# Score products of a sliding-window attention cut from 64x64 to 64x32 tiles of the TensorE array

## The chip, the cores and the metric

The kernel runs on one core of one Trainium2 chip. The metric is the device time of one execution in microseconds (us); lower is better. Times are medians over several runs, and profile pages and traces are of one profiled execution.

Five engines work side by side, each through its own list of instructions: PE (TensorE, matmuls; its weight loads are listed as PEld), DVE (VectorE), ACT (ScalarE), POOL (GpSimd) and SP, which here issues most DMAs. They wait for each other through semaphores. Matmul results go to PSUM, from where DVE and ACT read them.

## The reference

Two independent parts fill the two halves of the output's columns.

- **A, attention.** `x` is 2048x576. `qkv = x @ wqkv`, 32 heads of 18 features. Scores `q·k * 18**-0.5` are kept where `0 <= query - key < 256`; softmax over the keys, product with `v`, heads concatenated, `@ wo`.
- **B, a long convolution.** A filter of 2048 taps for each of 576 channels is computed from 128 complex exponentials, and `u` is convolved with it by Fourier transforms of length 4096; `u * Dskip` is added.

```python
scores = jnp.einsum("bhqd,bhkd->bhqk", q, k) * (Dh ** -0.5)
mask = (idx[:, None] - idx[None, :] >= 0) & (idx[:, None] - idx[None, :] < W)   # W = 256
p = _softmax(jnp.where(mask[None, None], scores, -1e9), axis=-1)
o = jnp.einsum("bhqk,bhkd->bhqd", p, v)
```

## The kernel before

The program has no loops at run time: Python writes every instruction out. Work is split into streams (generators), and the strings of `PLAN` give by hand the order in which the streams take their steps; each engine meets its instructions in that order. There are four stretches: `front` and `tables` (about 0 to 400 us: projections of q, k, v; the tables of the convolution filter), then `first` and `rest` (attention, the convolution's transforms, and the product with `wo`).

Attention is cut into 16 sets `i`: four chunks `c` of 512 queries by four groups `o` of eight heads. For a set, `Q` (128 x 4 x 512), `K` (128 x 4 x 768; 256 keys of the chunk before, and 512 of its own) and `V` are loaded. Heads sit at partitions 0 to 63 and 64 to 127 (index `r`), four to each (indices `b`, `pp`). q and k are kept as a high and a low float16 part, so that a head has 54 rows (and a 55th for its maximum).

Three streams use them:

- `smax` (letter `s` of the plan, method `smax1`): for every block of 64 queries (`qb`) and every `pp`, one **slot** of PSUM (`ring`, three buffers of 128 x 2 x 512) gets the scores of four heads: queries on PSUM's partitions, their keys along the free axis, 320 of them (64 queries and the 256 keys before), fewer at the start of the sequence. Four matmuls (L832) with `Q` as the weights, then four more (L840, or L843 at the start of the sequence) that add -3e38 through an identity `idb` where a key may not be seen. DVE then takes the maximum of each row (L866). After 16 slots the 128 x 32 maxima are transposed (L848) and written by DMA into the 55th row of `Q`.
- `scores` (`a`, method `score1`): the same scores turned round, keys on the partitions and queries along the free axis, 55 rows, so that the maximum is subtracted by the product itself. A slot holds one to three key blocks (table `TB`), four matmuls each (L917, `K` as the weights), masks (L926), and ACT's exponential (L932), which leaves `P` in SBUF.
- `pv` (`v`): the product of `V` and `P`, float32, on tiles of 64 rows by 32 columns (L952), into `po`.

The slice `z = 64 * (r ^ b)` puts the four matmuls of a group on four different quarters (64x64) of PE's array. The convolution's steps, which the plan sets between these, are L671 (64 rows by 32 columns), L704 (32 by 64) and L765 (128 by 64). A group of matmuls here is a set of them on different tiles of the array, issued one behind the other.

```python
for b in range(2):
    for r in range(2):
        z = 64 * (r ^ b)
        rr = slice(64 * r, 64 * r + 54)
        nc.tensor.matmul(ps[z:z + 64, b, :n], d["Q"][rr, 2 * b + pp, 64 * qb:64 * qb + 64],
                         d["K"][rr, 2 * b + pp, k0:k1], start=True, stop=False, skip_group_check=True)
```

Of the kernel before, what the change touches and what calls it, by code (L numbers as in the profile page):

```python
# [42 lines left out]
def constants():  # L43
    c = {}
    tau = 2 * np.pi
    l1, l2, f1, f2 = np.arange(64), np.arange(32), np.arange(64), np.arange(32)
    ph = -tau * np.outer(l1, f1 + 0.25) / 64
    m = np.stack([np.cos(ph), np.sin(ph)], 2).reshape(64, 128)
    wu = np.concatenate([m, m])
    wk = np.tile(m.reshape(32, 2, 128), (4, 1, 1))  # L50
    w2 = np.zeros((2, 2, 32, 8, 2, 2, 64))
    i1 = np.zeros((4, 32, 8, 2, 2, 64))
    for f in range(64):
        t, s, b = f // 8, f // 4 % 2, f % 4
        ph = -tau * np.outer(l2, f + 0.25 + 64 * f2) / 2048
        co, si = np.cos(ph), np.sin(ph)
        q, r = b // 2, b % 2
        w2[r, 0, :, t, s, q] = np.concatenate([co, si], 1)
        w2[r, 1, :, t, s, q] = np.concatenate([-si, co], 1)
        i1[b ^ s, :, t, s, 0] = np.concatenate([co.T, -si.T], 1)  # L60
        i1[b ^ s, :, t, s, 1] = np.concatenate([si.T, co.T], 1)
    ph = tau * np.outer(f1 + 0.25, l1) / 64
    i2 = np.stack([np.cos(ph), -np.sin(ph)], 1) / 2048
    i2 = i2[[f ^ (f // 4 % 2) for f in range(64)]].reshape(128, 64)
    mult = {"c_cm": np.arange(64), "c_ct": np.arange(32) + 0.5, "c_ca": np.r_[64 * np.arange(8), 512 * np.arange(4)],
            "c_cp": np.r_[np.zeros(8), np.full(4, 31.5)]}
    for nm, v in mult.items():
        t = np.zeros((3, GC, GC, len(v)))
        for g in range(GC):
            t[:, g, g] = v  # L70
        c[nm] = t.reshape(96, GC, len(v))
    big = -3e38
    p, x = np.arange(64)[:, None], np.arange(64)[None]
    sm = np.concatenate([np.where(x <= p, big, 0), np.where(x > p, big, 0)], 1)
    far, near, no = np.where(x >= p, big, 0), np.where(p > x, big, 0), np.zeros((64, 64))
    tm = np.concatenate([far, near, near, far, far, no], 1)
    c["c_sm"], c["c_tm"] = np.concatenate([sm, sm]), np.concatenate([tm, tm])
    c["c_if"] = np.eye(128)
    c["c_id"] = np.concatenate([np.eye(64), np.eye(64)])
    c["c_wu"], c["c_wk"], c["c_w2"], c["c_i1"], c["c_i2"] = wu, wk, w2.reshape(128, 8, 256), i1.reshape(128, 8, 256), i2  # L80
    half = ("c_sm", "c_tm", "c_id", *mult)
    return {k: np.ascontiguousarray(v.astype(ml_dtypes.bfloat16 if k in half else np.float32)) for k, v in c.items()}
# [48 lines left out]
class Kernel:  # L131
# [667 lines left out]
    def load(self, i):  # L799
# [7 lines left out]
        t0 = 0 if c else 4  # L807
        nc.sync.dma_start(d["V"][:, t0 * 76:912], self.vd[o, :, :, 8 * c - 4 + t0:8 * c + 8].rearrange("r k t e -> (r k) (t e)"))

    def smax(self):  # L810
        for i in range(16):
            yield from self.smax1(i)

    def smax1(self, i):
        nc, (c, o), d = self.nc, divmod(i, 4), self.sets[i % 3]
        yield "PE", (d["K"],), lambda: self.loaded > i
        m = self.p["m"].tile([128, 32], F32, name="m")
        mv = m.rearrange("p (b s) -> p b s", b=2)
        for qb in range(8):
            k0 = max(64 * qb, 256 if c == 0 else 0)  # L820
            k1 = 64 * qb + 320
            n = k1 - k0
            full = n == 320
            for pp in range(2):
                if qb or pp:
                    yield "PE", (d["K"],), "ring"
                ps = self.slot()
                for b in range(2):
                    for r in range(2):
                        z = 64 * (r ^ b)  # L830
                        rr = slice(64 * r, 64 * r + 54)
                        nc.tensor.matmul(ps[z:z + 64, b, :n], d["Q"][rr, 2 * b + pp, 64 * qb:64 * qb + 64],  # L832
                                         d["K"][rr, 2 * b + pp, k0:k1], start=True, stop=False, skip_group_check=True)
                for b in range(2):
                    for r in range(2):
                        z = 64 * (r ^ b)
                        rr = slice(64 * r, 64 * r + 64)
                        if full:
                            out = ps[z:z + 64, b, :320].rearrange("p (t x) -> p t x", x=64)[:, 0:5:4]
                            nc.tensor.matmul(out, self.idb[rr], self.sm[rr], start=False, stop=True,  # L840
                                             skip_group_check=True)
                        else:
                            nc.tensor.matmul(ps[z:z + 64, b, n - 64:n], self.idb[rr], self.sm[rr, 64:],  # L843
                                             start=False, stop=True, skip_group_check=True)
                self.post("2", (ps,), lambda out=mv[:, :, 8 * pp + qb], x=ps[:, :, :n]: self.red(out, x))
        yield "PE", (m,), "ring", lambda: self.n["max"] >= 16 * i + 16
        mt = self.slot()
        nc.tensor.transpose(mt[:32, 0, :128], m, self.idf)  # L848

        def go():  # L850
            m16 = self.p["m"].tile([32, 128], F16, name="m16")
            nc.vector.tensor_scalar(m16, mt[:32, 0, :128], 2.0 ** -15, None, op0=OP.mult)
            q = d["Q"].rearrange("(h r) p n -> h r (p n)", h=2)[:, 54]

            def store():
                for b in range(2):
                    src = m16[16 * b:16 * b + 16].rearrange("s (h x) -> h s x", h=2)
                    for r in range(2):
                        nc.sync.dma_start(q[r:r + 1, 1024 * b:1024 * b + 1024].rearrange("o (s x) -> o s x", x=64),
                                          src[r ^ b])  # L860
                self.maxed = i + 1
            self.post("4", (m16,), store)
        self.post("6", (mt,), go)
# [42 lines left out]
    def score1(self, bl, d, pp, Ps):  # L906
        nc = self.nc
        ps = self.slot()
        lo = min(x[1] for x in bl)
        hi = max(x[1] + x[3] for x in bl)  # L910
        for k, (rel, off, q0, w) in enumerate(bl):
            for b in range(2):
                for r in range(2):
                    z = 64 * (r ^ b)
                    rr = slice(64 * r, 64 * r + 55)
                    kc = 64 * (rel + 4)
                    nc.tensor.matmul(ps[z:z + 64, b, off:off + w], d["K"][rr, 2 * b + pp, kc:kc + 64],  # L917
                                     d["Q"][rr, 2 * b + pp, q0:q0 + w], start=(k == 0), stop=False,
                                     skip_group_check=True)
        for blk, kinds in self.masks(bl):  # L920
            w = 64 * len(kinds)
            for b in range(2):
                for r in range(2):
                    z = 64 * (r ^ b)
                    rr = slice(64 * r, 64 * r + 64)
                    nc.tensor.matmul(ps[z:z + 64, b, 64 * blk:64 * blk + w], self.idb[rr],  # L926
                                     self.tm[rr, self.MO[kinds]:self.MO[kinds] + w], start=False, stop=True,
                                     skip_group_check=True)

        def go():  # L930
            P = self.p["P"].tile([128, 2, 512], F32, name="P")
            nc.scalar.activation(P[:, :, lo:hi], ps[:, :, lo:hi], AF.Exp, scale=self.esc)  # L932
            Ps.append(P)
        self.post("1", (ps,), go)
# [253 lines left out]
```

## Time and profile before

| | |
|---|---|
| median of 3 runs | 882.83 us (879.99 to 886.74) |
| profiled execution | span of 879.6 us; the runs lie 0.4 to 7.1 us above it, the median 3.2 |
| PE busy | 722.6 us (82%), 14234 matmuls and as many weight loads |
| DVE busy | 600.4 us (68%) |
| ACT busy | 522.5 us (59%) |
| POOL busy | 378.4 us (43%) |
| bytes moved by DMA | 150.79 MB, 171 GB/s over the span |

A profile page lists busy times of each engine and the groups of instructions behind them; the trace can be asked for the rows of a stretch of time, in which an idle time ahead of an instruction stands in brackets with what ended it. "issue" there means that the profile shows nothing that the engine waited for. A matmul's end is modelled, so that busy times of PE hold the way through the array as well; starts are what can be compared.

### The profile page before, as it was taken

How to read it: one execution, taken by the hardware profiler on the slowest of the kernel's cores; microseconds unless marked ns; L12 is line 12 of the kernel's file. 1: busy time of each engine (PE TensorE's matmuls, PEld its weight loads, DVE VectorE, ACT ScalarE, POOL GpSimd, SP SyncE). 2: the span in 40 equal slices, each digit the busy share in tenths (PEclk: the TensorE clock that was granted, in tenths of full speed). 3: DMA queues.
4: the chain of work that ended last, by engine and by line, in shares of the span. 5: the costliest groups of instructions: out<-in, count | busy, mean ns of one | idle time of the engine just before them, and what ended most of it. 6: DMA issues, size and time to landing. Idle time of an engine off the chain costs nothing.

```text
span 879.6 us, 32028 instructions
## 1 busy us (share of the span) xinstructions
PE 722.6 (82%) x14234; PEld 439.6 (50%) x14234; DVE 600.4 (68%) x797; ACT 522.5 (59%) x685; POOL 378.4 (43%) x296
## 2 busy tenths in 40 slices
PE   4565957998889789887888897778888998999986
PEld 2321523456446545465555454445555555567655
DVE  6866887887987787768767787376776778861010
ACT  3247675678777857671465565545666676676431
POOL 2266867766687655665015132032133042332020
PEclk9885969999999999995899989889999999899998
DMA  9795261557247745468559568627557684855844
GB/s 313 263 231 129 66 155 37 138 104 180 55 110 196 152 116 159 101 158 238 149 180 286 183 202 248 180 78 241 169 153 212 200 245 121 257 159 171 239 144 140
DMA packets 210763, 150.79 MB, mean 171 GB/s; under 512 B 102538, under 2 KB 191242, under 8 KB 210368
## 3 DMA queue, kind: packets, MB, share of 16 engines
q1 hardware_dynamic: 208608, 144.74, 58.2%
q0 software_dynamic: 2016, 3.99, 1.5%
q8 instruction: 112, 1.84, 0.9%
q14 instruction: 27, 0.22, 0.1%
HBM read 83.44 MB, written 65.11 MB: 169 GB/s over the span
## 4 chain that ended last, share of the span: by engine, by line
PE 49%; DVE 16%; ACT 13%; issue 11%; DMA 5%; POOL 3%; SPq 3%; ACTq 0%; DVEq 0%; POOLq 0%
PE pp L174 10%; PE po L952 7%; PE ring L174 6%; ACT P L932 5%; PE ring L917 4%; PE ring L704 4%; DVE m L866 4%; PE ring L832 3%; PE ring L671 3%; PE ring L571 2%; PE ring L449 2%; PE ring L461 2%; PE ring L765 2%; PE ring L926 1%; DVE m L548 1%
## 5 line engine op out<-in xcount | busy, mean ns | idle before, releaser
L866 DVE TENSOR_REDUCE m<-ring 128x2 f32<-128x640 f32 (+4 forms) x256 | 187.4, 779 | 59.1 <-PE ring L840 55.4
L932 ACT ACTIVATE P<-ring,esc 128x1024 f32<-128x1024 f32 (+2 forms) x160 | 166.8, 1060 | 99.2 <-PE ring L926 91.1
L542 POOL TENSOR_TENSOR m<-A,tr 128x1024 f32<-128x1024 f32 x72 | 144.0, 2019 | 78.0 <-DVE m L548 66.9
L952 PE MATMUL po<-P,V 64*32 64x320 f32 (+4 forms) x2816 | 103.4, 368 | 3.3 <-issue 3.3
L832 PE MATMUL ring<-K,Q 54*64 54x320 f16 (+4 forms) x1024 | 83.3, 327 | 23.3 <-DMA K<-kz 7.1
L986 POOL TENSOR_TENSOR osb<-osb,T 128x1024 f32<-128x1024 f32 x16 | 37.8, 2364 | 99.9 <-DVE T L981 72.4
L692 POOL TENSOR_TENSOR Y<-t,t 128x384 f32<-128x384 f32 x24 | 24.0, 1001 | 131.4 <-DVE t L687 125.4
L832 PEld LDWEIGHTS <-Q 54*64 54x64 f16 x1024 | 43.4, 111 | 69.5 <-issue 61.3
L917 PE MATMUL ring<-Q,K 55*64 55x320 f16 (+4 forms) x1408 | 68.2, 273 | 12.0 <-ACT P L932 3.2
L994 POOL TENSOR_TENSOR oh<-osb,oh 128x1024 f16<-128x1024 f32 x16 | 34.2, 2135 | 72.4 <-ACT oh L990 72.4
L174 PE MATMUL pp<-xh,wh 128*128 128x512 f16 x180 | 48.3, 400 | 18.7 <-ACT vst L361 9.4
L174 PEld LDWEIGHTS <-wh 128*128 128x128 f16 x324 | 31.8, 102 | 57.1 <-issue 18.1
L840 PE MATMUL ring<-sm,idb 64*64 64x128 bf16 x896 | 56.7, 231 | 1.3 <-issue 1.2
L548 DVE TENSOR_TENSOR m<-m,m 128x1024 f32<-128x1024 f32 x36 | 53.4, 1482 | 4.8 <-POOL m L542 4.7
L571 PE MATMUL ring<-Q,m 128*32 128x64 f32 x2304 | 42.6, 231 | 16.1 <-DVE m L548 13.4
L917 PEld LDWEIGHTS <-K 55*64 55x64 f16 x1408 | 33.8, 111 | 41.1 <-issue 32.9
L952 PEld LDWEIGHTS po<-P,V 64*32 64x32 f32 x2816 | 38.7, 108 | 30.7 <-issue 21.3
L571 PEld LDWEIGHTS ring<-Q,m 128*32 128x32 f32 x2304 | 36.9, 117 | 29.6 <-issue 11.9
L174 PE MATMUL pp<-xh,wl 128*128 128x512 f16 x180 | 49.7, 411 | 0.0
L977 DVE STREAM_TRANSPOSE T<-osb 128x1024 f32<-128x1024 f32 x16 | 19.8, 1235 | 42.3 <-ACT osb L962 42.2
L926 PE MATMUL ring<-tm,idb 64*64 64x128 bf16 (+1 forms) x1152 | 45.0, 215 | 3.7 <-issue 3.7
L523 POOL TENSOR_TENSOR tr<-tr,mab 128x768 f32<-128x768 f32 x18 | 33.6, 1868 | 31.1 <-ACT tr L518 31.0
(162 smaller groups left out, 1568.2 us busy)
## 6 DMA issues: line engine op xcount, KB each, us to landing
gx<-ust SPq DMA_DIRECT2D x16, 576.0 KB
gk<-kst SPq DMA_DIRECT2D x18, 512.0 KB
tx<-gx SPq DMA_DIRECT2D x24, 384.0 KB
tk<-gk SPq DMA_DIRECT2D x24, 384.0 KB
h<-ho SPq DMA_DIRECT2D x48, 192.0 KB
hp<-h SPq DMA_DIRECT2D x12, 768.0 KB
Q<-qz SPq DMA_DIRECT2D x16, 512.0 KB
K<-kz SPq DMA_DIRECT2D x16, 512.0 KB
```

What stands on the lines that cost most here:

```text
L174: self.nc.tensor.matmul(ps, u, v, start=(i == 0), stop=(i == len(ops) - 1))
L542: tt(m[part], A[:, ch, a0:a0 + 8].unsqueeze(3).to_broadcast(sh), tr[:, ch, part, 0:8].unsqueeze(2).to_broadcast(sh), op=OP.mult)
L548: self.nc.vector.tensor_tensor(m[0], m[0], m[1], op=OP.add)
L571: nc.tensor.matmul(kp[32 * st:32 * st + 32, j, :], m[:, ch, 32 * term:32 * term + 32], Q[:, ch, term, :], start=(term == 0), stop=(term == ...
L832: nc.tensor.matmul(ps[z:z + 64, b, :n], d["Q"][rr, 2 * b + pp, 64 * qb:64 * qb + 64], d["K"][rr, 2 * b + pp, k0:k1], start=True, stop=Fals ...
L840: nc.tensor.matmul(out, self.idb[rr], self.sm[rr], start=False, stop=True, skip_group_check=True)
L866: self.nc.vector.tensor_reduce(out, x, axis=AX.X, op=OP.max)
L917: nc.tensor.matmul(ps[z:z + 64, b, off:off + w], d["K"][rr, 2 * b + pp, kc:kc + 64], d["Q"][rr, 2 * b + pp, q0:q0 + w], start=(k == 0), st ...
L926: nc.tensor.matmul(ps[z:z + 64, b, 64 * blk:64 * blk + w], self.idb[rr], self.tm[rr, self.MO[kinds]:self.MO[kinds] + w], start=False, stop ...
L932: nc.scalar.activation(P[:, :, lo:hi], ps[:, :, lo:hi], AF.Exp, scale=self.esc)
L952: nc.tensor.matmul(po[32 * p:32 * p + 32, z, q0:q0 + w], V[64 * z:64 * z + 64, kb * 76 + 19 * p:kb * 76 + 19 * p + 32], P[p % 2][64 * z:64 ...
L986: nc.gpsimd.tensor_tensor(osb, osb, rb, op=OP.mult)
```

## The change

The four matmuls of a group become eight: each 64-wide block of weights is cut into two of 32 (index `h`), so that a group covers eight tiles of 64 rows by 32 columns, the shape that the products with `V` have. The order in a group is given by `TILES`.

- `smax1`: each half of a query block takes its own 288 keys (32 queries and the 256 before) instead of the 320 of the whole block. The mask matmuls write 2 x 32 columns of each half instead of 2 x 64. DVE's maximum runs over 288 columns. At the start of the sequence (`full` false) the keys stay as they were.
- `score1`: each key block of 64 becomes two of 32 for the same queries; the masks' weights are 32 columns of `idb`, their columns as before.
- `constants`: the table `c_sm` of the masks gets the two 32-wide parts ahead of its old second half.

The plan, the slots, the loads, and the orders of DVE, ACT, POOL and SP stay as they were.

```diff
-    sm = np.concatenate([np.where(x <= p, big, 0), np.where(x > p, big, 0)], 1)
+    y = x[:, :32]
+    sm = np.concatenate([np.where(y <= p % 32, big, 0), np.where(y > p % 32, big, 0), np.where(x > p, big, 0)], 1)
...
+    TILES = [(b, r, h) for b in range(2) for h in range(2) for r in range(2)]
...
-                for b in range(2):
-                    for r in range(2):
-                        z = 64 * (r ^ b)
-                        rr = slice(64 * r, 64 * r + 54)
-                        nc.tensor.matmul(ps[z:z + 64, b, :n], d["Q"][rr, 2 * b + pp, 64 * qb:64 * qb + 64],
-                                         d["K"][rr, 2 * b + pp, k0:k1], start=True, stop=False, skip_group_check=True)
...
+                for b, r, h in self.TILES:
+                    z, rr, q0 = 64 * (r ^ b) + 32 * h, slice(64 * r, 64 * r + 54), 64 * qb + 32 * h
+                    k0 = q0 if full else 256
+                    nc.tensor.matmul(ps[z:z + 32, b, :n], d["Q"][rr, 2 * b + pp, q0:q0 + 32],
+                                     d["K"][rr, 2 * b + pp, k0:k0 + n], start=True, stop=False, skip_group_check=True)
+                for b, r, h in self.TILES:
+                    z, rr, hh = 64 * (r ^ b) + 32 * h, slice(64 * r, 64 * r + 64), slice(32 * h, 32 * h + 32)
+                    if full:
+                        out, mk = ps[z:z + 32, b, :288].rearrange("p (t x) -> p t x", x=32)[:, 0:9:8], self.sm[rr, :64]
+                    else:
+                        out, mk = ps[z:z + 32, b, n - 64:n], self.sm[rr, 64:]
+                    nc.tensor.matmul(out, self.idb[rr, hh], mk, start=False, stop=True, skip_group_check=True)
...
-                    nc.tensor.matmul(ps[z:z + 64, b, off:off + w], d["K"][rr, 2 * b + pp, kc:kc + 64],
-                                     d["Q"][rr, 2 * b + pp, q0:q0 + w], start=(k == 0), stop=False,
-                                     skip_group_check=True)
+            for b, r, h in self.TILES:
+                z, rr, kc = 64 * (r ^ b) + 32 * h, slice(64 * r, 64 * r + 55), 64 * (rel + 4) + 32 * h
+                nc.tensor.matmul(ps[z:z + 32, b, off:off + w], d["K"][rr, 2 * b + pp, kc:kc + 32],
+                                 d["Q"][rr, 2 * b + pp, q0:q0 + w], start=(k == 0), stop=False, skip_group_check=True)
```

PE's list shows it at the end of two slots of `smax` that stand between two steps of `pv` (`po` is what `pv` writes, `sm` the mask's table; the sizes are partitions by columns of the result). Before:

```order
L840 MATMUL ring<-sm,idb 64x2x64
L840 LDWEIGHTS idb
L840 MATMUL ring<-sm,idb 64x2x64
L952 MATMUL po<-P,V_4393 32x192 x8
L832 LDWEIGHTS Q_4387
L832 MATMUL ring<-K_4388,Q_4387 64x320
```

After the change, at the same place (the line numbers of `pv` move from L952 to L942):

```order
L840 MATMUL ring<-sm,idb 32x2x32
L840 LDWEIGHTS idb
L840 MATMUL ring<-sm,idb 32x2x32
L942 MATMUL po<-P,V_4393 32x192 x8
L832 LDWEIGHTS Q_4387
L832 MATMUL ring<-K_4388,Q_4387 32x288
```

Between the `pv` step shown and the one ahead of it stood 32 rows of `smax`; now there are 64. Results of 64 partitions beside those of 32 stood there before; now all have 32. In PE's whole list there were 226 places where a score matmul of 64 columns stood next to one of `pv` or L671 with 32.

At a slot of `scores` in the same stretch, from the block of 64 columns to that of 320, before:

```order
L917 MATMUL ring<-Q_4395,K_4396 64x64
L917 LDWEIGHTS K_4396
L917 MATMUL ring<-Q_4395,K_4396 64x64
L917 LDWEIGHTS K_4396
L917 MATMUL ring<-Q_4395,K_4396 64x320
```

and after (`score1` moves from L917 to L910):

```order
L910 MATMUL ring<-Q_4395,K_4396 32x64
L910 LDWEIGHTS K_4396
L910 MATMUL ring<-Q_4395,K_4396 32x64
L910 LDWEIGHTS K_4396
L910 MATMUL ring<-Q_4395,K_4396 32x320
```

The widths stay, and each stands eight times instead of four. Over the program the score and mask matmuls go from 4608 to 9216, each with its weight load: 9216 more instructions on PE.

More of the change, by code (lines that the diff above doesn't have):

```diff
@@ L819, in smax1 @@
         for qb in range(8):
[L820 to L823, printed above, removed]
+            full = c > 0 or qb >= 4
+            n = 288 if full else 64 * qb + 64
             for pp in range(2):
@@ L827, in smax1 @@
                 ps = self.slot()
-                for b in range(2):
-                    for r in range(2):
-                        z = 64 * (r ^ b)
-                        rr = slice(64 * r, 64 * r + 54)
-                        nc.tensor.matmul(ps[z:z + 64, b, :n], d["Q"][rr, 2 * b + pp, 64 * qb:64 * qb + 64],
-                                         d["K"][rr, 2 * b + pp, k0:k1], start=True, stop=False, skip_group_check=True)
[L834 to L840, printed above, removed]
-                                             skip_group_check=True)
-                        else:
-                            nc.tensor.matmul(ps[z:z + 64, b, n - 64:n], self.idb[rr], self.sm[rr, 64:],
-                                             start=False, stop=True, skip_group_check=True)
+                for b, r, h in self.TILES:
[10 more added lines that the diff above has]
+                    nc.tensor.matmul(out, self.idb[rr, hh], mk, start=False, stop=True, skip_group_check=True)
                 self.post("2", (ps,), lambda out=mv[:, :, 8 * pp + qb], x=ps[:, :, :n]: self.red(out, x))
@@ L911, in score1 @@
         for k, (rel, off, q0, w) in enumerate(bl):
[L912 to L917, printed above, removed]
-                                     d["Q"][rr, 2 * b + pp, q0:q0 + w], start=(k == 0), stop=False,
-                                     skip_group_check=True)
+            for b, r, h in self.TILES:
+                z, rr, kc = 64 * (r ^ b) + 32 * h, slice(64 * r, 64 * r + 55), 64 * (rel + 4) + 32 * h
+                nc.tensor.matmul(ps[z:z + 32, b, off:off + w], d["K"][rr, 2 * b + pp, kc:kc + 32],
+                                 d["Q"][rr, 2 * b + pp, q0:q0 + w], start=(k == 0), stop=False, skip_group_check=True)
         for blk, kinds in self.masks(bl):
             w = 64 * len(kinds)
[L922 to L928, printed above, removed]
+            for b, r, h in self.TILES:
+                z, rr = 64 * (r ^ b) + 32 * h, slice(64 * r, 64 * r + 64)
+                nc.tensor.matmul(ps[z:z + 32, b, 64 * blk:64 * blk + w], self.idb[rr, 32 * h:32 * h + 32],
+                                 self.tm[rr, self.MO[kinds]:self.MO[kinds] + w], start=False, stop=True,
+                                 skip_group_check=True)
         def go():
```

## The prediction

> **What bounds the kernel now.** I read the head of the page and its chain first, then busy times by stretch, then single stops of PE in the timeline.
>
> ```profile
> span 879.6 us, 32028 instructions
> PE 722.6 (82%) x14234; PEld 439.6 (50%) x14234; DVE 600.4 (68%) x797; ACT 522.5 (59%) x685; POOL 378.4 (43%) x296
> ...
> PE 49%; DVE 16%; ACT 13%; issue 11%; DMA 5%; POOL 3%; SPq 3%; ACTq 0%; DVEq 0%; POOLq 0%
> ```
>
> PE is the busiest engine and half of the chain that ended last. A tenth of that chain is "issue": time in which nothing was waited for that the profile knows. The change touches attention alone, so its stretch counts. Busy times by stretch (time, instructions of each engine in brackets; the three numbers at the end are PE's granted clock, DMA share and GB/s):
>
> ```profile
> 0.00:400.00 400.00, 311.01 (x3704) 176.68 (x3704) 308.66 (x407) 261.08 (x407) 252.04 (x212) 0.91 0.58 150
> 400.00:800.00 400.00, 343.19 (x9766) 214.27 (x9774) 286.42 (x386) 235.06 (x247) 117.36 (x81) 0.92 0.64 191
> 800.00:880.00 80.00, 68.36 (x772) 48.62 (x756) 5.34 (x6) 26.39 (x32) 8.97 (x4) 0.96 0.58 181
> ```
>
> From 400 to 800 us PE is busy for 86% of the time, DVE for 72%, ACT for 59%. PE runs 19,540 instructions there (9766 matmuls, 9774 loads), against 7408 in the 400 us before. What is its idle time? Around 546 us, four equal mask matmuls of one group:
>
> ```profile
> 545.70 0.14 PEld L926 LDWEIGHTS <-idb 64*64 64x64 bf16 x4
> 545.81 0.25 PE L926 MATMUL ring<-tm,idb 64*64 64x128 bf16 x3
> 548.79 0.21 PE L926 MATMUL ring<-tm,idb 64*64 64x128 bf16 x1 [2.73 <-issue]
> ```
>
> Three ran, the fourth stopped for 2.73 us, with its weights loaded and no semaphore between it and its sisters. It was not there yet: **PE waited for its own instructions.** They come by a DMA queue of their own. The queues of the whole page, and of 400 to 800 us alone (packets, MB, share):
>
> ```profile
> q8 instruction: 112, 1.84, 0.9%
> ```
>
> ```profile
> q8 instruction: 76, 1.25, 1.3%
> ```
>
> 112 packets for 28,468 instructions of PE are 254 each, 76 for 19,540 are 257: a packet holds 256. The first and the last of the 21 such stops of the stretch, 18.8 us in all:
>
> ```profile
> 450.67 0.73 PE L952 MATMUL po<-P,V 64*32 64x320 f32 x28 [0.60 <-issue]
> ...
> 785.55 0.72 PE L704 MATMUL ring<-Y,i 32*64 32x192 f32 x12 [0.40 <-issue]
> ```
>
> Each lies a whole multiple of 256 instructions from the next. From one stop's end to that of a later one, and some blocks of 256 that ran with no stop or a short one:
>
> ```profile
> 542.03:548.79 6.76, 3.75 (x128) 2.49 (x128) 3.37 (x4) 2.12 (x2) 1.95 (x2) 1.00 1.05 339
> 673.45:678.66 5.21, 3.20 (x128) 2.31 (x128) 1.99 (x3) 4.11 (x5) 1.70 (x2) 1.00 0.94 263
> 678.66:685.42 6.76, 6.11 (x128) 3.25 (x128) 4.58 (x6) 3.18 (x3) 2.33 (x2) 0.75 1.09 349
> 703.89:707.91 4.02, 3.70 (x129) 2.58 (x128) 3.66 (x5) 2.30 (x4) 1.88 (x1) 1.00 0.64 187
> 782.01:785.55 3.54, 3.14 (x129) 2.48 (x129) 3.37 (x5) 2.87 (x4) 1.24 (x2) 1.00 0.85 252
> 736.16:739.63 3.47, 3.21 (x133) 2.19 (x128) 2.77 (x4) 2.71 (x3) 0.00 (x0) 1.00 0.04 6
> 669.56:673.45 3.89, 3.54 (x140) 2.24 (x138) 2.45 (x4) 3.86 (x4) 0.00 (x0) 1.00 0.76 203
> 502.30:508.15 5.85, 5.11 (x126) 2.98 (x129) 4.03 (x6) 1.82 (x3) 0.00 (x0) 0.71 0.12 34
> ```
>
> Between two stops stand just 128 matmuls and 128 loads. So one block is fetched while the one ahead of it runs, and no more than one; a block can't take less time than the fetch of the next. The fetch took 6.76 us where the DMA share was 1.05 to 1.09, 5.21 at 0.94, 4.02 at 0.64, and 3.54 at the quickest with a stop (782.01): it stands behind the data's packets. No block of the stretch ran in under 3.47 us. The present mean is 400 / 76.3 blocks (19,540 / 256) = 5.24 us: work sets most blocks, the fetch some.
>
> **What the change takes away.** Starts in the timeline give PE's own price. A slot's mask group followed by the next slot on the same tile shape, and one followed by `pv`:
>
> ```profile
> 503.16 0.23 PE L926 MATMUL ring<-tm,idb 64*64 64x64 bf16 x8
> 503.23 0.31 PE L832 MATMUL ring<-K,Q 54*64 54x320 f16 x4
> 503.37 0.23 PE L840 MATMUL ring<-sm,idb 64*64 64x128 bf16 x4
> 503.44 0.33 PE L832 MATMUL ring<-K,Q 54*64 54x320 f16 x4
> ...
> 510.53 0.33 PE L832 MATMUL ring<-K,Q 54*64 54x320 f16 x4
> 510.67 0.25 PE L840 MATMUL ring<-sm,idb 64*64 64x128 bf16 x4
> 510.85 0.50 PE L952 MATMUL po<-P,V 64*32 64x320 f32 x8
> ```
>
> From mask to the next group: 0.07 us without a change of shape (503.37 to 503.44), 0.18 with one (510.67 to 510.85): about 0.1 us a change. 226 such neighbours become equal: 226 x 0.1 = 23 us. Four matmuls of 320 columns take 0.14 us from start to start (510.53 to 510.67), so 0.42 ns a column; 32 columns less in 224 slots is 0.013 x 224 = 3 us. A mask of 64 columns instead of 128 is 64 x 0.42 = 27 ns less; I take 20, since it is short: 0.02 x 224 = 4.5 us. Eight matmuls on eight tiles side by side I cost as one group's time, since the row of L952 has eight of 64x32 within 0.50 us. If their issue counted instead, eight would take 0.07 us with their loads (503.16 to 503.23: eight mask matmuls): under the 0.14 of a product, and for the masks as much as now, so that the 4.5 us would be gone. The gains are 23 + 3 + 4.5 = **30 us of PE work** (25 without the masks').
>
> DVE's maxima lose 64 of 640 elements:
>
> ```profile
> L866 DVE TENSOR_REDUCE m<-ring 128x2 f32<-128x640 f32 x224 | 174.1, 821 | 56.9 <-PE ring L840 55.4
> ...
> L866 DVE TENSOR_REDUCE m<-ring 128x2 f32<-128x512 f32 x8 | 5.2, 684 | 0.0
> ```
>
> (821 - 684) / 128 = 1.07 ns an element, 64 x 1.07 = 68 ns, x 224 = 15 us of DVE. But DVE waited 55.4 us for PE's slots (same row): I count none of it on the path.
>
> **What the change adds.** The rows of the four score groups carry the count, 4608 matmuls with L843's 128:
>
> ```profile
> L832 PE MATMUL ring<-K,Q 54*64 54x320 f16 (+4 forms) x1024 | 83.3, 327 | 23.3 <-DMA K<-kz 7.1
> ...
> L917 PE MATMUL ring<-Q,K 55*64 55x320 f16 (+4 forms) x1408 | 68.2, 273 | 12.0 <-ACT P L932 3.2
> ...
> L840 PE MATMUL ring<-sm,idb 64*64 64x128 bf16 x896 | 56.7, 231 | 1.3 <-issue 1.2
> ...
> L926 PE MATMUL ring<-tm,idb 64*64 64x128 bf16 (+1 forms) x1152 | 45.0, 215 | 3.7 <-issue 3.7
> ```
>
> They double: 4608 matmuls and 4608 loads more, 9216 / 256 = 36 more blocks. The stretch goes from 76.3 to 112.3 blocks. If work alone counted, a block would hold (400 - 18.8 - 30) / 112.3 = 3.1 us of it: **less than any block of before took, and less than the quickest fetch.** The fetch becomes the bound on all blocks but those that hold mostly `pv` and convolution, whose rows keep their count (502.30: 5.85 us without a stop, at a DMA share of 0.12).
>
> What does a block cost then? Lower end: the mean of the three shortest rows, (3.47 + 3.54 + 3.89) / 3 = 3.63 us. Upper end: a stretch in which the fetch already shares the bound, since 10 of the 21 stops lie in it:
>
> ```profile
> 640.00:720.00 80.00, 70.37 (x2113) 42.14 (x2108) 58.76 (x76) 52.76 (x53) 24.94 (x16) 0.98 0.68 207
> ```
>
> 4221 / 256 = 16.5 blocks, 80 / 16.5 = 4.85 us. The same bytes in a stretch a fifth longer bring the DMA share from 0.64 to some 0.53, so the rows of 0.64 and 0.76 (4.02 and 3.89) are nearest, not those around 1; the blocks with long work of their own pull the mean up. I take 4.3 us: 112.3 x 4.3 = 483 us for the stretch, **+83**. Lower end 112.3 x 3.63 = 408, +8; upper end 112.3 x 4.85 = 545, +145. The 30 us are hidden in this: PE's work ends ahead of the next block either way. The profiled span of 879.6 becomes 963; the median of the runs lies 3.2 above the span, so 966.
>
> DVE, ACT and SP get no new work; they wait for PE longer. The 0.6 MB of new instructions (9216 of 28,468 x 1.84 MB) are nothing among 150.79.
>
> **Rivals.**
>
> *The fetch keeps up* (7%). If a fetch could run several blocks ahead, only PE's work would count: 882.8 - 30 = 853 us, and 834 if the stops went too. For it: the tile shapes really cost 0.1 us at each change, and most of today's blocks run without a stop. Against it: the stops at every 256th instruction, and none of the shown blocks under 3.47 us. The Trainium skill (Runtime: NRT & Kernel Launch, Instruction fetch mechanics) takes this side: it has blocks of 16 KiB or 256 instructions, as the packets here, but says that the fetch is hidden because instructions are issued more slowly than they are filled in. The 2.73 us of the row above speak against that part; by that rule the time would be the 853 of this rival.
>
> *The fetch falls to its floor* (5%). With DMA spread thinner every block might cost 3.5 us (the row at 782.01): 112.3 x 3.5 = 393, -7, or 876: no change that can be told, since this kernel's runs show about 1% either way.
>
> *A fetch slower than I take* (6%, over 1030). The new packets crowd the loads of `K`, `V` and the spectra, and blocks stay at 5.2 us as at 673.45: 112.3 x 5.2 = 584, or 1067. Against it: the bytes are the same and the time longer.
>
> **How the numbers follow.** The forecast's case has 82%, its range from 891 (+8) to 1028 (+145), rounded to 890 and 1030. What lies outside is the first rival, most of the second and the third, 18% in all. Faster by over 1%: 7%, the first rival. Within 1%: 5%, the second. Slower: 88%.
>
> **What would show it.** In the new profile PE should have some 148 packets on the instruction queue, "issue" should lead PE's idle time from 400 us on with around a hundred us instead of 19, stops at multiples of 256 instructions, and no block under 3.4 us. From mask to `pv` 0.07 to 0.1 us should pass instead of 0.18, and L866's mean should be near 753 ns. DVE and ACT should wait longer for PE, at the same busy times but for DVE's 15 us. I am wrong if blocks of 256 run in under 3 us, if the stretch after 400 us has long stops elsewhere, or if the eight matmuls of a group start further apart than their columns take.

## The result, and the profile after

The changed kernel takes **988.2 us** (985.46 to 991.76) against 884.8 us of before (879.99 to 888.07) in the same comparison: a ratio of 1.117, 95% interval 1.113 to 1.122. The forecast was 966, with a range of 890 to 1030. Medians here and below are of all runs, ratios of the undisturbed ones.

The page of the changed kernel, its head, its instruction queue and its chain:

```profile
span 985.0 us, 41244 instructions
...
PE 744.5 (76%) x18842; PEld 479.6 (49%) x18842; DVE 590.4 (60%) x797; ACT 523.3 (53%) x685; POOL 377.9 (38%) x296
...
q8 instruction: 148, 2.42, 1.1%
...
PE 31%; issue 10%; ACT 4%; DVE 2%; DMA 2%; SPq 1%; ACTq 0%; POOL 0%; DVEq 0%
```

PE has 4608 more matmuls and as many more loads, and they cost its busy time 22 us only; the span grew by 105. (The chain's shares add up to half the span, so I do not read it further.) The instruction queue moved 148 packets, 36 more. Busy times of the two halves that the prediction compared, and of attention from its first maxima to its last product with `V`, in the changed kernel and then in before:

```profile
0.00:400.00 400.00, 311.98 (x3752) 177.73 (x3753) 310.15 (x408) 260.95 (x407) 252.95 (x212) 0.91 0.58 151
400.00:800.00 400.00, 283.82 (x11263) 195.64 (x11256) 222.20 (x316) 181.28 (x191) 88.88 (x62) 0.81 0.54 159
...
399.50:938.50 539.00, 398.17 (x14898) 278.49 (x14898) 277.44 (x387) 252.31 (x265) 120.94 (x83) 0.82 0.54 158
```

```profile
400.10:835.60 435.50, 378.35 (x10290) 239.75 (x10290) 288.82 (x388) 251.51 (x265) 121.75 (x83) 0.93 0.65 194
```

The first 400 us are the same. Attention went from 435.5 to 539.0 us: 103.5 of the 105 us. Of these, 84 us are idle time of PE and 20 us busy time. PE, DVE and ACT are all busy for a smaller share of it. PE's stops, the first and the last of 71 that lie whole multiples of 256 instructions apart, 105 us in all:

```profile
406.95 0.43 PE L832 MATMUL ring<-K,Q 54*32 54x288 f16 x4 [1.21 <-issue]
...
894.21 0.27 PE L916 MATMUL ring<-tm,idb 64*32 64x128 bf16 x13 [1.69 <-issue]
```

In before the same count gives 20 stops of 18.8 us (the prediction says 21; and of these 8, not 10, lie between 640 and 720 us). The stops grew by 87 us. The packets of the instruction queue show what ends them: at each of the 71, a packet of 16,384 bytes ended 1.0 to 1.6 us before PE went on (median 1.4). PE's 72 other waits after 400 us (of 0.15 us and more) end anywhere from 0.1 to 11.6 us behind one. One of the stops, in the middle of a group of eight mask matmuls:

```profile
447.81 0.42 PE L832 MATMUL ring<-K,Q 54*32 54x288 f16 x8
448.03 0.22 PE L840 MATMUL ring<-sm,idb 64*32 64x64 bf16 x6
449.92 0.20 PE L840 MATMUL ring<-sm,idb 64*32 64x64 bf16 x2 [1.66 <-issue]
449.92 0.32 PE L832 MATMUL ring<-K,Q 54*32 54x288 f16 x8
450.06 0.22 PE L840 MATMUL ring<-sm,idb 64*32 64x64 bf16 x8
```

Six of the eight ran, and the other two started 1.89 us after the first of these. Blocks from the end of one stop to the end of the next (length; instructions; the last three numbers are granted clock, DMA share, GB/s):

```profile
470.08:476.00 5.92, 2.56 (x128) 1.58 (x128) 5.03 (x7) 1.91 (x2) 0.00 (x0) 0.66 0.89 264
604.31:610.93 6.62, 3.93 (x128) 3.15 (x129) 0.82 (x2) 2.95 (x3) 0.00 (x0) 0.74 1.08 354
647.50:653.98 6.48, 3.87 (x128) 2.46 (x128) 4.89 (x6) 1.11 (x1) 0.83 (x1) 0.50 0.91 306
750.16:753.90 3.74, 2.39 (x128) 1.58 (x128) 2.09 (x3) 1.95 (x2) 0.00 (x0) 0.72 0.02 4
558.77:562.72 3.95, 3.15 (x127) 1.85 (x127) 3.03 (x5) 1.93 (x2) 1.11 (x1) 1.00 0.39 120
629.67:633.15 3.48, 2.70 (x127) 1.83 (x128) 2.96 (x6) 2.12 (x2) 3.22 (x2) 1.00 0.02 5
```

128 matmuls and 128 loads in each. With the DMA engines idle (0.02) a block still needs 3.48 or 3.74 us, and near a full share 5.92 to 6.62. PE's own part of such a block is 2.4 to 3.9 us. Between two neighbouring stops no block took less than 3.47 us, but a block behind a long step can pass faster. Behind two steps of the convolution (L705, L766), the block from 855.27 on took 2.09 us for some 128 matmuls and as many loads:

```profile
855.27:857.36 2.09, 2.04 (x140) 1.62 (x129) 1.78 (x3) 1.33 (x2) 0.98 (x1) 1.00 0.03 3
```

What keeps its distance is the fetch: no two packets of the queue start less than 3.3 us apart.

What the other engines show:

```profile
L862 DVE TENSOR_REDUCE m<-ring 128x2 f32<-128x576 f32 x224 | 162.5, 756 | 140.0 <-PE ring L840 138.4
...
L922 ACT ACTIVATE P<-ring,esc 128x1024 f32<-128x1024 f32 (+2 forms) x160 | 166.9, 1060 | 172.3 <-PE ring L916 161.9
```

A maximum takes 756 ns instead of 821, and DVE waits 140 us for PE ahead of them instead of 57. ACT's exponentials take what they took, and wait 162 us for the score slots instead of 91.

### The profile page after: what moved, and what is told of

It reads as the page before. It is cut to its first block, busy times and chain, and to the rows that moved or that the text cites. A ratio compares the mean times of both kernels' runs of the same rounds, so it can differ in the third digit from the quotient of the medians.

```text
span 985.0 us, 41244 instructions
## 1 busy us (share of the span) xinstructions
PE 744.5 (76%) x18842; PEld 479.6 (49%) x18842; DVE 590.4 (60%) x797; ACT 523.3 (53%) x685; POOL 377.9 (38%) x296
## 4 chain that ended last, share of the span: by engine, by line
PE 31%; issue 10%; ACT 4%; DVE 2%; DMA 2%; SPq 1%; ACTq 0%; POOL 0%; DVEq 0%
PE po L942 6%; PE ring L175 6%; PE ring L705 4%; PE ring L910 4%; ACT P L922 3%; PE ring L672 3%; PE ring L832 3%; PE ring L916 2%; PE ring L766 2%; DVE m L862 1%; DMA oh<-od 1%; PE ring L840 1%; DMA Q<-m 1%; ACT ho L712 0%; SPq L855 0%
## 5 line engine op out<-in xcount | busy, mean ns | idle before, releaser
L862 DVE TENSOR_REDUCE m<-ring 128x2 f32<-128x576 f32 (+4 forms) x256 | 176.0, 722 | 146.9 <-PE ring L840 145.1
L942 PE MATMUL po<-P,V 64*32 64x320 f32 (+4 forms) x2816 | 123.4, 408 | 6.7 <-issue 6.5
L832 PE MATMUL ring<-K,Q 54*32 54x288 f16 (+2 forms) x2048 | 95.1, 328 | 40.6 <-issue 16.0
L910 PE MATMUL ring<-Q,K 55*32 55x320 f16 (+4 forms) x2816 | 85.3, 292 | 33.7 <-issue 18.8
L840 PE MATMUL ring<-sm,idb 64*32 64x64 bf16 x2048 | 71.8, 215 | 23.4 <-issue 23.4
L832 PEld LDWEIGHTS <-Q 54*32 54x32 f16 x2048 | 49.2, 99 | 75.5 <-issue 69.9
L916 PE MATMUL ring<-tm,idb 64*32 64x128 bf16 (+1 forms) x2304 | 62.5, 234 | 25.7 <-issue 25.7
L910 PEld LDWEIGHTS <-K 55*32 55x32 f16 x2816 | 48.0, 100 | 53.1 <-issue 43.7
L942 PEld LDWEIGHTS po<-P,V 64*32 64x32 f32 x2816 | 53.0, 119 | 19.8 <-issue 16.2
L916 PEld LDWEIGHTS <-idb 64*32 64x32 bf16 x2304 | 42.9, 105 | 30.6 <-issue 27.9
L840 PEld LDWEIGHTS <-idb 64*32 64x32 bf16 x2048 | 40.0, 97 | 27.1 <-issue 26.1
```

The lines of the kernel that those rows point to most:

```text
L832: nc.tensor.matmul(ps[z:z + 32, b, :n], d["Q"][rr, 2 * b + pp, q0:q0 + 32], d["K"][rr, 2 * b + pp, k0:k0 + n], start=True, stop=False, ski ...
L840: nc.tensor.matmul(out, self.idb[rr, hh], mk, start=False, stop=True, skip_group_check=True)
L862: self.nc.vector.tensor_reduce(out, x, axis=AX.X, op=OP.max)
L910: nc.tensor.matmul(ps[z:z + 32, b, off:off + w], d["K"][rr, 2 * b + pp, kc:kc + 32], d["Q"][rr, 2 * b + pp, q0:q0 + w], start=(k == 0), st ...
L916: nc.tensor.matmul(ps[z:z + 32, b, 64 * blk:64 * blk + w], self.idb[rr, 32 * h:32 * h + 32], self.tm[rr, self.MO[kinds]:self.MO[kinds] + w ...
L942: nc.tensor.matmul(po[32 * p:32 * p + 32, z, q0:q0 + w], V[64 * z:64 * z + 64, kb * 76 + 19 * p:kb * 76 + 19 * p + 32], P[p % 2][64 * z:64 ...
```

## The experiments

The theory: PE's instructions arrive in blocks of 256, one block ahead, so that blocks can't follow each other faster than their fetches; the change adds 36 blocks. The rival that would leave the same result: groups on 64x32 tiles run slower on PE. What the runs gave, by the packets on the instruction queue. The last column counts PE's idle times after 400 us for which the profile names no releaser; it misses one stop each of before and the change, for which ACT or DVE is named, and counts one more in before:

| run | packets | us | ratio to before (95%) | idle times, us |
|---|---|---|---|---|
| e8: before, no masks | 95 | 859.3 | 0.972 (0.968 to 0.976) | 6, 3.1 |
| e11: before, no masks in `smax` | 104 | 873.8 | 0.985 (0.980 to 0.990) | 11, 9.8 |
| before | 112 | 884.3 to 887.0 | 1 | 20, 17.3 |
| e4: change, no masks | 114 | 889.0 | 1.000 (0.995 to 1.004) | 26, 38.4 |
| e5: 64x64, columns halved, no masks | 114 | 894.9 | 1.013 (1.009 to 1.017) | 23, 24.4 |
| e2: change in `smax` alone | 128 | 925.0 | 1.046 (1.039 to 1.054) | 45, 59.0 |
| e12: change, no masks in `smax` | 132 | 935.7 | 1.056 (1.051 to 1.062) | 45, 65.0 |
| e3: change in `scores` alone | 132 | 938.8 | 1.061 (1.056 to 1.066) | 46, 63.4 |
| the change | 148 | 988.2 | 1.117 (1.113 to 1.122) | 70, 104.1 |
| e1: 64x64, columns halved | 148 | 990.5 | 1.116 (1.108 to 1.123) | 61, 95.7 |

The runs of e4 lie between 879.5 and 898.7 us, and its profiled execution took 892.9.

**e1: the number of instructions without the shape.**

```diff
-                        nc.tensor.matmul(ps[z:z + 64, b, :n], d["Q"][rr, ..., 64 * qb:64 * qb + 64],
-                                         d["K"][rr, 2 * b + pp, k0:k1], start=True, stop=False, ...)
+                        for x0, x1 in ((0, n // 2), (n // 2, n)):
+                            nc.tensor.matmul(ps[z:z + 64, b, x0:x1], d["Q"][rr, ..., 64 * qb:64 * qb + 64],
+                                             d["K"][rr, 2 * b + pp, k0 + x0:k0 + x1], start=True, stop=False, ...)
```

and the same for L840, L843, L917 and L926.

> The tiles of before (64x64), but every score product and every mask is cut into two of half the columns: the same 9216 more instructions on PE as the change has, none of its tile shapes. Theory, the fetch of instructions: 148 packets on the instruction queue and 980 to 1010 us, like the change (988), with some 60 to 80 stops after 400 us. Rival, the 64x32 groups themselves run slower on PE: close to before, 885 to 900 us, with some 20 stops.

990.5 us. Attention, and one stop:

```profile
402.20:947.70 545.50, 425.66 (x14898) 294.66 (x14898) 291.79 (x387) 252.86 (x265) 120.07 (x83) 0.86 0.53 156
```

```profile
701.97 0.41 PE L932 MATMUL ring<-tm,idb 64*64 64x64 bf16 x11
703.05 0.27 PE L932 MATMUL ring<-tm,idb 64*64 64x64 bf16 x2 [0.67 <-issue]
```

The same 14,898 matmuls and loads, the same stops in the middle of a group, and the same time within the error, on the tiles of before. With idle times of 96 us against 104, the shape is not what costs.

**e2 and e3: each half of the change alone.** `smax1` of the change with `score1` of before, and the other way round.

> The change in smax alone, scores as before: 4096 more instructions. Theory: 128 packets, 905 to 930 us. Rival (a shape that runs slower): no tie to the packets; one half of the change carries nearly all of the 103 us, so that this one is either under 890 or over 970 us.

> The change in scores alone, smax as before: 5120 more instructions. Theory: 132 packets, 920 to 950 us, above the run with smax alone. Rival: as there, under 890 or over 970 us, the other way round.

925.0 and 938.8 us, both in their ranges. 16 blocks cost 39 us and 20 cost 53 (each against the 885.9 of their comparison), 36 cost 103: 2.4, 2.65 and 2.9 us a block. Neither half carries the loss alone.

**e4 and e5: few instructions, both shapes.** e4 leaves L840, L843 and L916 out of the change; e5 leaves them out of e1.

```diff
-                for b, r, h in self.TILES:
-                    z, rr, hh = 64 * (r ^ b) + 32 * h, slice(64 * r, 64 * r + 64), slice(32 * h, 32 * h + 32)
...
-                    nc.tensor.matmul(out, self.idb[rr, hh], mk, start=False, stop=True, skip_group_check=True)
```

> The change with all mask matmuls left out (so the masking of scores and maxima is not computed): 64x32 tiles, but only 512 instructions more than before. Theory: 114 packets, 840 to 875 us, below before. Rival (64x32 groups run slower): the score products, over half of the groups, still have the shape, so 930 us or more.

> The tiles of before with score products cut into two of half the columns and all mask matmuls left out (masking is not computed): the same count of instructions as the run e4, on 64x64 tiles, with the changes of tile shape. Theory: within 15 us of e4, 840 to 880 us, since the fetch hides most of the 0.1 us a change. If changes of shape count in full, e5 is slower than e4 by some 20 to 30 us; if 64x32 groups run slower, it is faster by over 40 us.

Their order is as expected: the shape of the change is 6 us (medians) to 12 us (ratios) faster than 64x64 at an equal count of instructions, so 64x32 groups do not run slower. The level was **missed**: 889.0 and 894.9 instead of 840 to 880. I had taken the masks' work off the path; the time stayed that of before, whose packets they nearly share (114 to 112). The run to hold them against is e8 below, before without its masks: it has 95 packets and takes 859.3 us, so the 19 packets more cost 30 us on 64x32 tiles and 36 on 64x64.

**e8, e9, e10: what sets the time where the fetch does not?** e8 leaves all masks out of before. e9 and e10 halve DVE's maxima, in before and in the change:

```diff
-                self.post("2", (ps,), lambda out=mv[:, :, 8 * pp + qb], x=ps[:, :, :n]: self.red(out, x))
+                self.post("2", (ps,), lambda out=mv[:, :, 8 * pp + qb], x=ps[:, :, :n // 2]: self.red(out, x))
```

> Before with all mask matmuls left out and nothing split (masking is not computed): 4352 instructions on PE fewer than before, 95 packets. Theory P, PE's own work sets the time between stops: 805 to 835 us. Theory R, the round trip of a slot of PSUM (PE fills it, DVE or ACT empties it, three buffers) sets it: 865 to 890 us, with PE's waits for L866 and L932 longer than before.

> Before with DVE's maxima taken over the first half of a slot's columns only (the maxima are not those of all keys): some 77 us less on DVE, PE's list unchanged. Theory P: 875 to 890 us, as before. Theory R: 840 to 870 us.

> The change with the same halved maxima. Theory of the fetch: DVE's time counts for little there: 970 to 990 us, and less gained than in e9 if that one gains. Rival (slots bind here too): as many us gained as in e9, under 965 us if theory R holds there.

e8 took 859.3 us, between the ranges of P and R; both fell as they stood. e9 took 878.5, a ratio of 0.994 (0.992 to 0.997) and in P's range, and e10 987.1, a ratio of 1.117 (1.109 to 1.125), the change's own. The row of e9:

```profile
L866 DVE TENSOR_REDUCE m<-ring 128x2 f32<-128x320 f32 x224 | 104.6, 490 | 107.2 <-PE ring L840 104.9
```

70 us less of DVE's work became 50 us more of DVE's waiting for PE (107.2 instead of 56.9) and 6 us of time. So a slot's round trip is worth little in before and nothing in the change. In e8 PE had 17 blocks fewer and no mask work, PE's idle times without a releaser fell from 17.3 to 3.1 us, and the time by 25: some 14 of these are theirs, if nothing else moved. Work of PE that is taken away between stops does not come off one for one; what takes its place (slots, loads, the clock) was not separated.

**e6 and e7: does the fetch stand behind the data?** The convolution's `tx` and `tk` are loaded once.

```diff
-            x = fs.tile([128, 4, 192], F32, name=nm)
-            nc.sync.dma_start(x, g[8 * t:8 * t + 8, :, :, 192 * ch:192 * ch + 192]
+            if n == 0:
+                self.one[nm] = self.p["cc"].tile([128, 4, 192], F32, name=nm)
+                nc.sync.dma_start(self.one[nm], g[8 * t:8 * t + 8, :, :, 192 * ch:192 * ch + 192]
...
+            r.append(self.one[nm])
```

> Before, with the spectra's inputs tx and tk loaded once instead of 24 times (the convolution's output is that of the first inputs): some 18 MB less on the DMA queues after 400 us, the same instructions on PE. Theory: fetches wait less behind data, but bind little here: 865 to 880 us. Rival: the same step as in e7.

> The change with the same single load of tx and tk. Theory: fetches bind nearly every block and take less time: 925 to 965 us, a gain two to five times that of e6. Rival (the fetch doesn't stand behind the data's DMAs, or doesn't bind): the same gain as e6, 970 to 983 us.

873.4 us (0.985, 0.977 to 0.994) and 963.6 us (1.086, 1.078 to 1.094): gains of 12 and 25 us, twice as much in the change. Their stretches, e6 and e7:

```profile
400.00:800.00 400.00, 347.48 (x9904) 219.34 (x9905) 289.24 (x389) 240.25 (x252) 120.39 (x83) 0.93 0.51 150
```

```profile
400.00:800.00 400.00, 283.98 (x11815) 203.06 (x11823) 231.40 (x330) 190.84 (x202) 98.30 (x70) 0.86 0.44 126
```

In e7 a block takes 400 / (23,638 / 256) = 4.33 us at a DMA share of 0.44, against 400 / (22,519 / 256) = 4.55 at 0.54 in the change. That agrees with fetches that wait behind data, and the blocks above show it more plainly (3.5 us at a share of 0.02, 6.6 at 1.08). So do the packets of the changed kernel. At 23 of the 70 stops other queues hold less than a tenth of the DMA engines in the 1.2 us after PE goes on, and the next instruction packet starts 1.05 to 1.77 us after PE (median 1.2); at 30 stops they hold over nine tenths, and it starts 1.2 to 4.2 us after (median 2.8). The packet itself takes some 1.1 us either way. But e7's idle times without a releaser, 74 of 104 us, are those of the change (70 of 104), so this pair does not settle how much of the 25 us the fetch gave.

**e11 and e12: a version that is faster.** A softmax may be shifted by any number that is not below the largest score, so the maximum over all 320 keys of a slot serves as well, unseen ones among them. L840 and L843 go, out of before (e11) and out of the change (e12):

```diff
-                                         d["K"][rr, 2 * b + pp, k0:k1], start=True, stop=False, skip_group_check=True)
+                                         d["K"][rr, 2 * b + pp, k0:k1], start=True, stop=True, skip_group_check=True)
-                for b in range(2):
-                    for r in range(2):
...
-                            nc.tensor.matmul(out, self.idb[rr], self.sm[rr], start=False, stop=True,
-                                             skip_group_check=True)
...
```

> Before without the mask matmuls of smax alone (L840, L843): the shift of the softmax is then the maximum over all 320 keys of a slot, unseen ones too, which is never below the maximum wanted; what is left out is the masking of the maxima, the masking of the scores stays. 2048 instructions on PE fewer, 104 packets. Theory (the time goes by the packets, from 859 us at 95 and 885 at 112): 868 to 878 us. Rival (PE's fetch counts only in the change): 882 to 888 us.

> The change without the mask matmuls of smax, in the same way: 4096 instructions fewer than the change, 132 packets as in the run with the scores alone changed (939 us). Theory: 925 to 945 us. Rival (something in smax's 64x32 products costs, not the number): 965 us or more.

873.8 us, 1.5% under before (0.980 to 0.990), and 935.7 us, both as the packets had it. e12 has as many packets as e3, other instructions among them, and a time within 0.5% of it. The queue's row in e11:

```profile
q8 instruction: 104, 1.70, 0.8%
```

e11 beats both kernels. Its limit: an unseen key whose score lies far above all seen ones would make every term of a row tiny; inputs of that kind were not tried.

## Why the prediction was right

*Fetch of instructions as the bound.* Right. The stops at every 256th instruction, each just behind the end of a packet, show the fetch itself. Three comparisons show that the count and not the shape brings them: the same count on other tiles gives the same time (e1 and the change), other instructions of the same count do too (e3 and e12), and without masks a higher count costs 30 us on one shape and 36 on the other (e8 to e4 and to e5). That e4 is back at the level of before proves nothing by itself, since the masks' work is gone as well. A price of each instruction on PE itself would also rise with the count; it can be no more than a part, since 84 of the 103.5 us are idle time. The time rises with the packets throughout the table, and faster the more there are: 1.5 us a packet from 95 to 112 (the masks' work among it), 2.5 from 112 to 128, 3.2 from 132 to 148. That is as a fetch hidden behind work in some blocks, and in ever fewer, would have it.

*36 more blocks, 148 packets.* Exact.

*4.3 us a block.* Mis-sized, by 4 to 6%: the forecast was 483 us for 112.3 blocks, and with 103 instead of 83 us added it is 503, or 4.48; counted from 400 to 800 us it is the 4.55 above. The value was a choice between 3.63 and 4.85. The DMA share fell as I had it (0.54, forecast 0.53). A term that I left out is the clock: its granted share went from 0.93 to 0.82 over attention, and in blocks with long stops to 0.50 or 0.66. The products with `V`, the same in both kernels, show it, before and after:

```profile
L952 PE MATMUL po<-P,V 64*32 64x320 f32 (+4 forms) x2816 | 103.4, 368 | 3.3 <-issue 3.3
```

```profile
L942 PE MATMUL po<-P,V 64*32 64x320 f32 (+4 forms) x2816 | 123.4, 408 | 6.7 <-issue 6.5
```

They were busy for 20 us more. How much of the missing 20 us of the forecast the clock is, no run here separated, since slower work can hide behind the fetch.

*PE's work of 30 us less, hidden.* Right in that nothing of it shows in the change (988.2 against e1's 990.5). The step that the prediction cost at 23 us, the changes of tile shape, did become cheap. From mask to `pv`, 0.18 us before, 0.03 us pass in the change (forecast 0.07 to 0.1):

```profile
855.26 0.21 PE L840 MATMUL ring<-sm,idb 64*32 64x64 bf16 x8
855.29 0.61 PE L942 MATMUL po<-P,V 64*32 64x256 f32 x16
```

But the fetch covered it. At a small count (e4 against e5) shape and width together gave 6 to 12 us, less than half of the 30. A slip in the sum is without weight: 0.14 us over 320 columns are 0.44 ns a column, not 0.42.

*DVE's 15 us, off the path.* Right: 756 ns measured, 753 forecast; and another 68 us off DVE's busy time in e10 moved nothing (987.1 us).

*The rivals.* "The fetch keeps up" had 853 us. The stops speak against its condition. Its price is doubtful too: with almost no stops left and all masks' work gone, e8 still took 859, though on the tiles of before; no run had the change's tiles without the fetch. "The fetch falls to its floor" did not come: quiet blocks did fall to 3.5 us, but the loads come in bursts, and blocks of 6 us and more stayed. "A fetch slower than I take" was the side on which the result lies, short of its 1067. The rule of the Trainium skill (Runtime: NRT & Kernel Launch, Instruction fetch mechanics), that the fetch is hidden by the pace of issue, does not hold here (71 stops, 105 us); its block of 256 instructions does (36 more packets for 9216 more instructions).

*What would show it.* The packets, the stops at every 256th instruction (105 us; "around a hundred" forecast), and DVE and ACT waiting longer for PE: all as said. "No block under 3.4 us" was put too strongly. It holds between neighbouring stops (3.47 us and more); behind a long step blocks of 2 to 3 us occur, as from 855.27 on. The prediction took such a block for a sign of being wrong. But the packet for the block behind it had started some 0.4 us before this block did. What was never under 3.3 us is the time from packet to packet.

## What to carry to other kernels

Count PE's instructions as a resource: between stops, 256 of them cost 3.5 us at best here and over 6 while data moves, so cutting matmuls into smaller tiles pays only while a block of 256 holds clearly more work than that. The sign to look for is an idle time with no releaser in the middle of a group of equal matmuls, at a fixed multiple of instructions, just behind a packet of the instruction queue. Where PE is at that edge, leaving instructions out (masks that a maximum does not need: 52 us from the change to e12) gains more than making each one quicker (2 us from e1 to the change, within the error).

## What was not expected of the hardware

PE's granted clock fell where it had more stops, from 0.93 to 0.82 over attention and to 0.50 in single blocks; that the stops are the cause was not tested. The work is slower at the lower clock: in the changed kernel neighbouring products with `V` of 320 columns start 46 ns apart on average at a clock of 0.50, and 26 ns at 1.00. And in before, 70 us of DVE's work (e9) and all of the mask matmuls (e8) were worth 6 and 25 us only: with DVE at 66% and PE at 87% of the stretch, neither was the bound alone.
